# Two 64-query attention tiles of neighbouring heads as one tile of 128 rows, in a fused attention and feed-forward kernel

## The chip, the cores and the metric

One core of one Trainium2 chip. The time is the device time of the whole program in microseconds (us). Three runs of the kernel before gave 1238.19, 1238.35 and 1239.01; their median, 1238.35, is the time before. One further execution was profiled.

## What is computed

Eight batches of eight heads, 576 positions, 64 numbers a head, all in float32. Each head's output mixes causal softmax attention with a linear memory; the mix is one input row of a two-layer feed-forward part with 512 inputs and 2048 hidden units.

```python
scores = q @ k.T / sqrt(64), causal;  a = softmax(scores);  local = a @ v
phi(x) = where(x > 0, x, exp(x) - 1) + 1
mem = (phi(q) @ M_prev) / (phi(q) @ z_prev + 1e-6)
g = 1 / (1 + exp(-beta))                  # one number a head
x = g * mem + (1 - g) * local             # heads side by side: 4608 x 512
out = leaky_relu(x @ w_in, 0.01) @ w_out  # 512 -> 2048 -> 512
```

## The kernel before

**Chunks and heads.** A batch's 576 queries are two chunks: chunk 0 has the first 320 queries (and needs the first 320 keys), chunk 1 the other 256 (and all 576 keys). Work goes unit by unit: batch `b`, chunk `hf`, head `h`. Chunk 0 has three tiles of 64, 128 and 128 query rows with 64, 192 and 320 keys; chunk 1 has two of 128 rows with 448 and 576 keys (`ROWS`, `KEYS`, lines 35 to 39).

**One head** (`attention`, line 361). One DMA loads a block `raw` of 128 partitions: transposed q and k, then M and v in blocks of 128 rows, z, and q by rows (line 355). The first two chunks, both of batch 0, are "plain" and compute in float32. All later ones split each operand into a high and a low part and multiply the parts with faster matmuls: ACT casts q and k (line 395), POOL makes the low part of q (line 402) and of k on 64 partitions (line 399), and the same for v (lines 408, 412). For each tile PE makes the scores with two matmuls (line 530) into `s`; DVE adds the mask and takes the row's minimum of the negated scores (line 534) into `pp`; ACT takes the exponential and its sum (line 550); DVE adds the gate to the sum, inverts it and scales the row (lines 555, 560, 563). POOL writes the memory part, phi(q) divided by its norm, into the first 64 columns of `pp` (line 566). Then PE transposes blocks of 128 columns of `pp` into `t` (line 479), ACT casts them into the high half of `pt` (line 494) and DVE subtracts for the low half (line 497). When all of the head's blocks are there, PE multiplies them with M and v (line 664) into `o`, and ACT, DVE and POOL make x and its low part from it (lines 667 to 676). The small chain on phi(q) (lines 433 to 452) runs beside this, for all tiles of a head at once.

**The 64-row tile.** Its scores are two matmuls of 64 columns, and its `pp` has 64 columns of memory part and 64 of probabilities, so its transpose is one block. A block of 128 rows, transposed, gives 128 columns of which the copies take 64 (`ROWS[0]`).

**Feed-forward part** (class `Moe`, line 688). For a chunk that is done: 16 steps, each with 12 matmuls into `h` and 12 into `acc` (line 699), over 320 or 256 columns, with the weights also split in high and low parts.

**Order.** Every instruction is recorded as an `op` with an engine, a duration from a small table, a priority and the tiles that it reads and writes. `Plan.issue` (line 127) then runs a list schedule over those durations and writes the program of each engine in that order; at run time each engine goes through its own list and waits on semaphores. Attention has the better priority; the feed-forward matmuls of the chunk before fill PE. `Buf` gives tiles in rings: two of `raw`, `qk`, `pp`, `pt` and the PSUM tile `t`, one of `vt`; a new user of a ring waits for the last reader of the one that had its place. An operation that DVE shares a port for is planned not to overlap with one of POOL (`port=True`).

Of the kernel before, what the change touches and what calls it, by code (L numbers as in the profile page):

```python
# [20 lines left out]
P = 128  # L21
# [11 lines left out]
RAWW = (320 + 320 + 3 * 64 + 64 + 3 * 64, 256 + 576 + 5 * 64 + 64 + 2 * 64)  # L33

# [184 lines left out]
def moe_attention(ctx, tc, raw0, raw1, beta, w_in, w_out, out, nb):  # L219
    nc = tc.nc  # L220
    rawd = (raw0, raw1)
    pool = lambda name, **kw: ctx.enter_context(tc.tile_pool(name=name, bufs=1, **kw))
# [57 lines left out]
    nc.vector.tensor_scalar(out=gate[:, 1, :], in0=gate[:, 1, :], scalar1=1.0e18, scalar2=None, op0=ALU.min)  # L280
    pts = []
# [65 lines left out]
    def load(b, hf, h, prio):  # L347
        args = [P, RAWW[1]], F32, "raw", 2, f"raw{b}_{hf}_{h}"
        if (b, hf) == (0, 0) and h % 2:
            r = c0_tile([P, RAWW[0]], F32, "rawc0", 2, args[4])  # L350
        elif (b, hf) == (0, 1) and h % 2:
            r = c1_tile(*args[:2], "rawc1", 1, args[4])
        else:
            r = tile_(*args)
        op("DMA", RAWW[hf] * 512 / 310, prio, lambda: nc.sync.dma_start(r()[:, : RAWW[hf]], rawd[hf][b, h]), w=[r[0]])
        raws[b, hf, h] = r

    xs = {}
    x32s = {}

    def attention(b, hf, h, prio):
        u = f"{b}_{hf}_{h}"
        nq, nk, tl, nj = NQ[hf], NK[hf], TILES[hf], NJ[hf]
        ni = len(tl)
        raw = raws.pop((b, hf, h))
        o_v, o_z, o_q = nq + nk, nq + nk + nj * D, nq + nk + nj * D + D

        full = plain(b, hf)
        if not full:
            qk = late_tile([P, 1088], F32R, "qk", 2, "qk" + u)  # L370
# [13 lines left out]
        else:  # L384

            pt = plan.buf(None, None, None, "pt", 2, None, behind["late"])
            pt.make = lambda at=pt.at: pt_tile(at % 2)
# [6 lines left out]
        def qk_hi():  # L394
            nc.scalar.copy(qk()[:, : nq + nk], raw()[:, : nq + nk])  # L395

        def k_lo():
            ks = slice(nq, nq + nk)
            nc.gpsimd.tensor_tensor(out=qk()[64:, ks], in0=raw()[64:, ks], in1=f32r_bits(qk()[64:, ks]), op=ALU.subtract)

        def q_lo():
            nc.gpsimd.tensor_tensor(out=qk()[:, nq + nk : nk + 2 * nq], in0=raw()[:, :nq], in1=f32r_bits(qk()[:, :nq]), op=ALU.subtract)
# [13 lines left out]
        else:  # L416
            operands = [qk["q"], qk["k"], qk["ql"]]
            op("ACT", act(nq + nk), prio, qk_hi, r=[raw[0]], w=[qk["q"], qk["k"]])
            op("POOL", pool_(nq), prio, q_lo, r=[raw[0], qk["q"]], w=[qk["ql"]])
            op("POOL", pool_(nk), prio, k_lo, r=[raw[0]], w=[qk["k"]])  # L420
# [20 lines left out]
        def phi_z():  # L441
            z = raw()[:, o_z:o_q].unsqueeze(1).to_broadcast([P, ni, D])
# [5 lines left out]
        def phi_den():  # L448
            nc.vector.tensor_scalar(out=rn(), in0=rn(), scalar1=1e-6, scalar2=gate[:, 0, h : h + 1], op0=ALU.add, op1=ALU.mult)
# [23 lines left out]
        def turns(ii, i, rw, n, pp):  # L473
            for j0, js in BLOCKS[i]:
# [6 lines left out]
                def part(x, js=js, i=i, rw=rw):  # L481
# [8 lines left out]
                def tv(t=t, js=js, rw=rw):  # L490
                    return t()[:, : len(js) * rw].rearrange("p (j q) -> p j q", q=rw)

                def p_hi(part=part, tv=tv):
                    nc.scalar.copy(part(0), tv())  # L494

                def p_lo(part=part, tv=tv):
                    nc.vector.tensor_tensor(out=part(1), in0=tv(), in1=f32r_bits(part(0)), op=ALU.subtract)  # L497
# [7 lines left out]
        for ii, i in enumerate(tl):  # L505
# [13 lines left out]
            for k, (k0, kc, kn) in enumerate(PIECES[i]):  # L519
                s = bank(("acc0", "s", "acc1")[i] if (b, hf) == (0, 0) else "s", 1, f"s{u}_{i}_{k}")  # L520

                def score(s=s, i=i, k0=k0, kc=kc, kn=kn):
                    if full:
# [3 lines left out]
                        return  # L527
                    for k in range(2):
                        c = COL[i] + k * (nq + nk)
                        nc.tensor.matmul(s()[:, :kc], qk()[:, c : c + P], qk()[:, nq + k0 : nq + k0 + kc], start=k == 0, stop=k == 1)  # L530

                def top(s=s, i=i, k=k, k0=k0, kn=kn, pp=pp, stat=stat):
                    mo = S - KEYS[i] + k0 if i else S - P
                    nc.vector.tensor_tensor_reduce(  # L534
                        out=pp()[:, D + k0 : D + k0 + kn],
                        in0=s()[:, :kn],
                        in1=mask[:, mo : mo + kn],
                        scale=-0.0625 if full else -0.125,
                        scalar=stat(k - 1) if k else 3.0e38,
                        op0=ALU.add,  # L540
                        op1=ALU.min,
                        accum_out=stat(k),
                    )

                op("PE", pe4(kn) if full else 2 * pe(kc), prio, score, r=operands, w=[s[0]])
                op("DVE", dve_top(kn) + 60 * (k > 0), prio, top, r=[s[0], st["m", ii, k - 1]], w=[pp["s", k], st["m", ii, k]])
# [7 lines left out]
            def inv(stat=stat):  # L554
                nc.vector.tensor_scalar(
                    out=stat(2), in0=stat(2), scalar1=1e-9, scalar2=gate[:, 1, h : h + 1], op0=ALU.add, op1=ALU.mult
                )
# [58 lines left out]
        blocks = [(i, j0) for i in tl for j0, _ in BLOCKS[i]]  # L616
# [43 lines left out]
        c0 = [min(0 if j < tl[0] or j == 0 else COL[j], nq - 192) for j in range(nj)]  # L660
# [152 lines left out]
def layout(q, k, v, M_prev, z_prev, beta, moe_w_in, moe_w_out):  # L813
# [9 lines left out]
    raw1 = np.concatenate([qT[..., 320:], kT, vx, zb, qx[..., 3 * D :]], -1)  # L823
    wi = moe_w_in.reshape(4, P, NF, P).transpose(2, 1, 0, 3).reshape(NF, P, DM)
# [29 lines left out]
```

## Time and profile before

| | before |
|---|---|
| median of 3 runs | 1238.35 us |
| the profiled execution, own time | 1238.4 us |
| its span, first to last instruction | 1236.6 us |
| PE busy | 1204.7 us (97%), 8936 matmuls |
| DVE, ACT, POOL busy | 827.7, 831.7, 707.4 us |
| bytes moved by DMA | 107.57 MB, mean 87 GB/s |

The engines run beside each other, so the busy times don't add up. PE is TensorE's matmuls, PEld its weight loads, DVE is VectorE, ACT ScalarE, POOL GpSimd, SP the engine that issues the DMAs. Matmuls are pipelined: the duration of one row runs into the next, so what one costs is read from starts. "Idle before" is the time an engine stood before an instruction, with the one that ended the wait.

### The profile page before, as it was taken

How to read it: one execution, taken by the hardware profiler on the slowest of the kernel's cores; microseconds unless marked ns; L12 is line 12 of the kernel's file. 1: busy time of each engine (PE TensorE's matmuls, PEld its weight loads, DVE VectorE, ACT ScalarE, POOL GpSimd, SP SyncE). 2: the span in 40 equal slices, each digit the busy share in tenths (PEclk: the TensorE clock that was granted, in tenths of full speed). 3: DMA queues.
4: the chain of work that ended last, by engine and by line, in shares of the span. 5: the costliest groups of instructions: out<-in, count | busy, mean ns of one | idle time of the engine just before them, and what ended most of it. 6: DMA issues, size and time to landing. Idle time of an engine off the chain costs nothing.

```text
span 1236.6 us, 25876 instructions
## 1 busy us (share of the span) xinstructions
PE 1204.7 (97%) x8936; PEld 1159.9 (94%) x8936; DVE 827.7 (67%) x2836; ACT 831.7 (67%) x2451; POOL 707.4 (57%) x1064
## 2 busy tenths in 40 slices
PE   6699999999999999999999999999999999999998
PEld 4488899999999999999999999999999999999998
DVE  6989877778687747767476775767567674776100
ACT  7877777777767757677576765767577775767322
POOL 1022276676776656666476665757666675766222
PEclk9999999999999999999999999999999999999999
DMA  6555322222323212222122221222122221222000
GB/s 248 185 177 171 126 95 82 85 86 74 98 69 108 73 47 93 76 96 73 59 87 76 91 73 59 90 86 78 55 81 90 86 73 48 93 79 74 1 22 18
DMA packets 32530, 107.57 MB, mean 87 GB/s; under 512 B 3728, under 2 KB 11920, under 8 KB 32400
## 3 DMA queue, kind: packets, MB, share of 16 engines
q1 hardware_dynamic: 32400, 105.92, 26.0%
q8 instruction: 71, 1.16, 0.4%
q14 instruction: 59, 0.48, 0.1%
HBM read 96.47 MB, written 9.44 MB: 86 GB/s over the span
## 4 chain that ended last, share of the span: by engine, by line
PE 88%; DVE 4%; ACT 4%; DMA 1%; POOL 1%; issue 1%; SPq 0%; POOLq 0%; DVEq 0%
PE acc L699 31%; PE h L699 31%; PE t L479 8%; PE o L664 8%; PE s L530 7%; PE o L628 2%; DMA raw<-raw 1%; PE s L526 1%; ACT pp L550 1%; DVE pp L534 1%; ACT gh L726 1%; ACT qk L395 1%; DVE pp L563 1%; ACT g L727 0%; DVE ph L439 0%
## 5 line engine op out<-in xcount | busy, mean ns | idle before, releaser
L732 POOL TENSOR_TENSOR gl<-g,gh 128x320 fp32r<-128x320 f32 (+1 forms) x256 | 210.3, 822 | 247.8 <-ACT g L727 220.8
L699 PE MATMUL h<-xh,wih 128*128 128x256 f32 (+1 forms) x1024 | 321.9, 314 | 3.7 <-ACT g L727 2.6
L699 PE MATMUL acc<-gh,woh 128*128 128x256 f32 (+1 forms) x1024 | 316.2, 309 | 0.0
L699 PE MATMUL h<-xl,wih 128*128 128x256 f32 (+1 forms) x1024 | 302.1, 295 | 0.4 <-DVE xl L648 0.4
L699 PE MATMUL h<-xh,wil 128*128 128x256 f32 (+1 forms) x1024 | 302.3, 295 | 0.0
L699 PE MATMUL acc<-gl,woh 128*128 128x256 f32 (+1 forms) x1024 | 301.5, 294 | 0.0
L699 PE MATMUL acc<-gh,wol 128*128 128x256 f32 (+1 forms) x1024 | 301.4, 294 | 0.0
L550 ACT ACTIVATE pp<-pp,st 128x448 f32<-128x448 f32 (+3 forms) x320 | 180.6, 565 | 85.2 <-DVE st L534 80.4
L699 PEld LDWEIGHTS h<-xh,wih 128*128 128x128 f32 x1024 | 194.1, 190 | 7.9 <-ACT g L727 4.2
L726 ACT ACTIVATE gh<-h 128x320 fp32r<-128x320 f32 (+1 forms) x256 | 104.8, 409 | 143.4 <-PE h L699 141.5
L699 PEld LDWEIGHTS h<-xl,wih 128*128 128x128 f32 x1024 | 194.1, 190 | 2.1 <-issue 0.9
L699 PEld LDWEIGHTS acc<-gl,woh 128*128 128x128 f32 x1024 | 193.3, 189 | 0.8 <-POOL gl L732 0.2
L699 PEld LDWEIGHTS acc<-gh,woh 128*128 128x128 f32 x1024 | 193.0, 188 | 0.8 <-issue 0.2
L699 PEld LDWEIGHTS h<-xh,wil 128*128 128x128 f32 x1024 | 193.1, 189 | 0.0
L699 PEld LDWEIGHTS acc<-gh,wol 128*128 128x128 f32 x1024 | 192.5, 188 | 0.0
L497 DVE TENSOR_TENSOR pt<-t,pt 128x256 fp32r<-128x256 f32 (+4 forms) x392 | 161.4, 428 | 37.7 <-ACT pt L494 34.5
L494 ACT CAST pt<-t 128x256 fp32r<-128x256 f32 (+4 forms) x392 | 142.2, 382 | 60.8 <-PE t L479 58.6
L479 PE MATMUL t<-ident,pp 128*128 128x128 f32 x960 | 169.4, 277 | 9.6 <-DVE pp L563 2.7
L534 DVE CUSTOM_DVE_ANT_0 pp<-s,mask 128x448 f32<-128x448 f32 (+3 forms) x320 | 137.7, 431 | 46.8 <-PE t L479 22.7
L563 DVE TENSOR_SCALAR pp<-pp,st 128x64 f32<-128x64 f32 (+4 forms) x280 | 150.5, 538 | 7.1
L530 PE MATMUL s<-qk 128*128 128x320 f32 (+4 forms) x672 | 151.5, 307 | 1.0 <-DVE st L534 0.2
L479 PEld LDWEIGHTS t<-ident,pp 128*128 128x128 f32 x960 | 116.4, 141 | 23.1 <-ACT pt L494 5.2
(67 smaller groups left out, 2042.7 us busy)
## 6 DMA issues: line engine op xcount, KB each, us to landing
raw<-raw SPq DMA_DIRECT2D x64, 672.0 KB, 4.0
raw<-raw SPq DMA_DIRECT2D x64, 544.0 KB, 3.6
wrwi<-w_in_bits SPq DMA_DIRECT2D x16, 512.0 KB, 3.5
wrwo<-w_out_bits SPq DMA_DIRECT2D x16, 512.0 KB, 3.6
out_t<-os SPq DMA_DIRECT2D x32, 160.0 KB, 1.8
out_t<-os SPq DMA_DIRECT2D x32, 128.0 KB, 1.8
braw<-beta_b SPq DMA_DIRECT2D x1, 4.0 KB, 1.6
```

The costliest lines, as they stand in the source:

```text
L479: nc.tensor.transpose(t()[:, (j - j0) * P : (j - j0 + 1) * P], pp()[:, j * P : (j + 1) * P], ident)
L494: nc.scalar.copy(part(0), tv())
L497: nc.vector.tensor_tensor(out=part(1), in0=tv(), in1=f32r_bits(part(0)), op=ALU.subtract)
L530: nc.tensor.matmul(s()[:, :kc], qk()[:, c : c + P], qk()[:, nq + k0 : nq + k0 + kc], start=k == 0, stop=k == 1)
L534: nc.vector.tensor_tensor_reduce(out=pp()[:, D + k0 : D + k0 + kn], in0=s()[:, :kn], in1=mask[:, mo : mo + kn], scale=-0.0625 if full else ...
L550: nc.scalar.activation(out=pp()[:, D : D + n], in_=pp()[:, D : D + n], func=AF.Exp, scale=-1.0, bias=stat(kl_), accum_out=stat(2))
L563: nc.vector.tensor_scalar(out=pp()[:, D : D + n], in0=pp()[:, D : D + n], scalar1=stat(2), scalar2=None, op0=ALU.mult)
L628: nc.tensor.matmul(o()[a, c0[j] : nq], v, pt()[:, 0, cols(j, c0[j]) : cols(j, nq)], start=j == 0, stop=j == nj - 1)
L664: nc.tensor.matmul(o()[:, c0[j] : nq], vt()[:, j, :], pt()[:, t, cols(j, c0[j]) : cols(j, nq)], start=n == 0, stop=n == len(mm) - 1)
L699: nc.tensor.matmul(dst(), l(), r(), start=start and k + j == 0, stop=stop and k + j == len(ops) - 1)
L726: op("ACT", act(n, True), q, lambda: nc.scalar.activation(out=gh()[:, :n], in_=hp()[:, :n], func=AF.Prelu, alpha=0.01), r=[hp[0]], w=[gh[0]])
L732: lambda: nc.gpsimd.tensor_tensor(out=gl()[:, :n], in0=g()[:, :n], in1=f32r_bits(gh()[:, :n]), op=ALU.subtract),
```

## The change

In the 320-query chunk of batches 1 to 7 (`paired`), the 64-query tile of an even head and that of the odd head behind it become one tile of 128 rows, worked on with the even head: the odd head's queries in rows 0 to 63, the even head's in rows 64 to 127. The host lays out a further input, `rawp`, one block for each pair of heads: the even head's block with the odd head's first 64 queries and keys put ahead of the even head's own, and three blocks of z. The even head loads this block (1344 columns where it loaded 1088), and its q and k parts are 384 columns long, not 320. The pair's scores are two matmuls of 128 columns, of which the off-diagonal quarters are not used; the mask and minimum go over each half of the rows by itself. One exponential, one scaling, one memory part and one transpose follow. The transposed block's columns are copied in two parts, to the even head's `pt` and to the odd head's. The even head takes its tiles in the order 1, 2, then the pair's; the odd head has tiles 1 and 2 alone. Two small constants hold the gates by halves of the rows, made by five copies at the start.

```diff
@@ layout, on the host
+    ev, od = slice(0, None, 2), slice(1, None, 2)
+    half = np.arange(P)[:, None] < D
+    zp = np.where(half, zb[:, od], zb[:, ev])
+    qp = np.where(half, qx[:, od, :, :D], np.roll(qx[:, ev, :, :D], D, 2))
+    rawp = np.concatenate(
+        [
+            *(qT[:, od, :, :D], qT[:, ev, :, :320], kT[:, od, :, :D], kT[:, ev, :, :320], vx[:, ev, :, : 3 * D]),
+            *(zp, zb[:, ev], zb[:, ev], qp, qx[:, ev, :, D : 3 * D]),
+        ],
+        -1,
+    )
@@ load
+        two = paired(b, hf) and h % 2 == 0
+        src, n = (rawp[b, h // 2], RAWP) if two else (rawd[hf][b, h], RAWW[hf])
@@ attention
+        if paired(b, hf) and h % 2:
+            tl = tl[1:]
...
+            pt = pairs.pop(b) if paired(b, hf) and h % 2 else new_pt()
+            if two:
+                pt2 = pairs[b] = new_pt()
...
-                op("ACT", act(nn, True), prio, p_hi, r=[t[0]], w=[pt["h", i, j0]])
-                if not full:
-                    op("DVE", dve(nn), prio, p_lo, r=[t[0], pt["h", i, j0]], w=[pt["l", i, j0]])
+                for to, c in ((pt, 64), (pt2, 0)) if two and i == 0 else ((pt, 0),):
...
+                    op("ACT", act(nn, True), prio, p_hi, r=[t[0]], w=[to["h", i, j0]])
+                    if not full:
+                        op("DVE", dve(nn), prio, p_lo, r=[t[0], to["h", i, j0]], w=[to["l", i, j0]])
+        order = list(enumerate(tl))
+        if two:
+            order = order[1:] + order[:1]
...
+                    c, w, n = (0, wq, P) if two and i == 0 else (q0 + COL[i], wq + k0_ + k0, kc)
                     for k in range(2):
-                        c = COL[i] + k * (nq + nk)
-                        nc.tensor.matmul(s()[:, :kc], qk()[:, c : c + P], qk()[:, nq + k0 : nq + k0 + kc], start=k == 0, stop=k == 1)
+                        ql = qk()[:, c + k * (wq + wk) : c + k * (wq + wk) + P]
+                        nc.tensor.matmul(s()[:, :n], ql, qk()[:, w : w + n], start=k == 0, stop=k == 1)
...
+                    for rs, c in ((slice(0, 64), 0), (slice(64, P), 64)) if two and i == 0 else ((slice(0, P), 0),):
+                        nc.vector.tensor_tensor_reduce(
+                            out=pp()[rs, D + k0 : D + k0 + kn],
+                            in0=s()[rs, c : c + kn],
+                            in1=mask[rs, mo + c : mo + c + kn],
...
```

The scheduler writes a new order behind the plain chunks. In the names below, `s_0_2_0_0` is chunk 0, head 2, tile 0, and the last number is a buffer's. PE, the scores of a small tile in the chunk 0 of batch 6, as they stand before (head 3's):

```order
L699 MATMUL h_0_10_13200<-xl_0_0_11253,wih_1306 128x320
L699 MATMUL h_0_10_13200<-xh_0_0_11239,wil_1310 128x320
L530 MATMUL s_0_3_0_0_13227<-qk_0_3_13151 128x64 x2
L479 MATMUL t_0_2_1_0_13234<-ident,pp_0_2_1_13161 128x128 x2
L699 MATMUL acc_0_0_12494<-gh_0_9_13170,woh_1270 128x320
L699 MATMUL acc_0_0_12494<-gl_0_9_13186,woh_1270 128x320
```

And with the change, in the same chunk, those of the pair of heads 2 and 3:

```order
L747 MATMUL acc_0_2_12320<-gl_0_8_12895,woh_1170 128x320
L747 MATMUL acc_0_2_12320<-gh_0_8_12882,wol_1181 128x320
L577 MATMUL s_0_2_0_0_12972<-qk_0_2_12849 128x128 x2
L747 MATMUL acc_0_3_12328<-gh_0_8_12882,woh_1170 128x320
L747 MATMUL acc_0_3_12328<-gl_0_8_12895,woh_1170 128x320
L747 MATMUL acc_0_3_12328<-gh_0_8_12882,wol_1181 128x320
L520 MATMUL t_0_2_1_0_12981<-ident,pp_0_2_1_12938 128x128 x2
```

Head 3 has no such row any more. In the whole program PE has 616 score matmuls for 672 and 932 transposes for 960; between a pair's scores and its transpose stand 18 to 48 feed-forward matmuls, and between the last products of the odd head before and that transpose 18 to 72.

DVE in the same chunk with the change, where the pair's tile goes through: two reductions of 64 rows, then one gate, one reciprocal and one scaling (its `pp_0_2_0`), beside the other tiles of heads 2 and 3:

```order
L583 ISA pp_0_2_0_12990,st_0_2_12912<-s_0_2_0_0_12972,mask 64x64
L583 ISA st_0_2_12912 64x1
L583 ISA pp_0_2_0_12990,st_0_2_12912<-s_0_2_0_0_12972,mask 64x64
L583 ISA st_0_2_12912 64x1
L542 TENSOR_TENSOR pt_1990<-t_0_2_1_0_12981,pt_1990 128x2x128
L484 TENSOR_REDUCE st_0_3_13006<-pz_0_3_12934 128x2
L605 TENSOR_SCALAR st_0_2_12912<-st_0_2_12912,gpair 128x1
L490 TENSOR_SCALAR st_0_3_13006<-st_0_3_13006,gate 128x2
L608 RECIPROCAL st_0_2_12912<-st_0_2_12912 128x1
L583 ISA pp_0_3_1_13018,st_0_3_13006<-s_0_3_1_0_13003,mask 128x192
L583 ISA st_0_3_13006 128x1
L611 TENSOR_SCALAR pp_0_2_0_12990<-pp_0_2_0_12990,st_0_2_12912 128x64
```

Before, each of the heads had its own such tile here, with one reduction of 128 rows, a gate, a reciprocal and a scaling.

## Rows read from the trace of the kernel before

**Rows 1.** The page's span, the busy time of each engine (share of the span, instructions), and the shares of the chain that ended last.
```profile
span 1236.6 us, 25876 instructions
PE 1204.7 (97%) x8936; PEld 1159.9 (94%) x8936; DVE 827.7 (67%) x2836; ACT 831.7 (67%) x2451; POOL 707.4 (57%) x1064
PE 88%; DVE 4%; ACT 4%; DMA 1%; POOL 1%; issue 1%; SPq 0%; POOLq 0%; DVEq 0%
```

**Rows 2.** The stretches view: 155 to 1154 us, from the end of the plain chunks to the end of the last attention. Columns: length, busy us and instructions of PE, PEld, DVE, ACT and POOL, granted clock, DMA share, GB/s.
```profile
155.00:1154.00 999.00, 991.77 (x7602) 975.98 (x7602) 696.72 (x2458) 689.76 (x2049) 657.50 (x997) 1.00 0.24 78
```

**Rows 3.** The waits of PE in that stretch, the longest sum: who waited for whom, us in total, times, the longest.
```profile
PE t L479 <- DVE pp L563: 2.7, 5, 0.6
```

**Rows 4.** Single rows in order of time (start, duration, engine, line): the last x of the 320-query chunks of batches 1 and 3 on POOL, and the first feed-forward matmuls of the chunks of batches 1, 3 and 7 on PE.
```profile
220.02 0.88 POOL L676 TENSOR_TENSOR xl<-x,xh 128x320 fp32r<-128x320 f32 x1
...
228.58 0.31 PE L699 MATMUL h<-xh,wih 128*128 128x320 f32 x1
...
498.20 0.88 POOL L676 TENSOR_TENSOR xl<-x,xh 128x320 fp32r<-128x320 f32 x1
...
527.52 0.30 PE L699 MATMUL h<-xh,wih 128*128 128x320 f32 x1
...
1114.44 0.31 PE L699 MATMUL h<-xh,wih 128*128 128x320 f32 x1
```

**Rows 5.** PE in order of time, three places: one transpose, two scores of 192 columns, two of 64 columns ("x2": two in one row), each between feed-forward matmuls of 320 columns. Between 443.37 and 446.74 there are only feed-forward matmuls, 23 steps.
```profile
429.50 0.31 PE L699 MATMUL acc<-gh,wol 128*128 128x320 f32 x1
429.65 0.27 PE L479 MATMUL t<-ident,pp 128*128 128x128 f32 x1
429.68 0.40 PE L699 MATMUL h<-xh,wih 128*128 128x320 f32 x1
429.91 0.31 PE L699 MATMUL h<-xl,wih 128*128 128x320 f32 x1
...
432.27 0.31 PE L699 MATMUL acc<-gh,wol 128*128 128x320 f32 x1
432.41 0.37 PE L530 MATMUL s<-qk 128*128 128x192 f32 x2
432.62 0.33 PE L699 MATMUL acc<-gh,woh 128*128 128x320 f32 x1
432.79 0.31 PE L699 MATMUL acc<-gl,woh 128*128 128x320 f32 x1
...
443.37 0.31 PE L699 MATMUL acc<-gh,woh 128*128 128x320 f32 x1
...
446.74 0.30 PE L699 MATMUL acc<-gh,wol 128*128 128x320 f32 x1
446.88 0.30 PE L530 MATMUL s<-qk 128*128 128x64 f32 x2
447.02 0.40 PE L699 MATMUL acc<-gh,woh 128*128 128x320 f32 x1
447.25 0.31 PE L699 MATMUL acc<-gl,woh 128*128 128x320 f32 x1
```

**Rows 6.** Groups of instructions by line and shape: count, busy us, mean ns of one, idle time before them. Score matmuls of 64 columns, and the weight loads of all score matmuls.
```profile
L530 PE MATMUL s<-qk 128*128 128x64 f32 x112 | 19.0, 252 | 0.2
L530 PEld LDWEIGHTS s<-qk 128*128 128x128 f32 x672 | 104.9, 189 | 6.0 <-DVE st L534 3.2 <-POOL pz L443 0.9 <-POOL qk L399 0.3
```

**Rows 7.** The same view, other engines: casts of q and k, low parts, exp and memory part of the 64-row tile (L566 has one shape for all tiles).
```profile
L395 ACT CAST qk<-raw 128x832 fp32r<-128x832 f32 x56 | 49.9, 890 | 8.2 <-DMA raw<-raw 8.2
L395 ACT CAST qk<-raw 128x640 fp32r<-128x640 f32 x56 | 40.7, 726 | 12.2 <-DMA raw<-raw 11.3 <-PE acc L699 0.8
L399 POOL TENSOR_TENSOR qk<-raw,qk 64x320 fp32r<-64x320 f32 x56 | 49.5, 884 | 4.4
L402 POOL TENSOR_TENSOR qk<-raw,qk 128x320 fp32r<-128x320 f32 x56 | 49.2, 879 | 29.6 <-ACT qk L395 25.0 <-PE t L479 2.8 <-PE o L664 0.6
L402 POOL TENSOR_TENSOR qk<-raw,qk 128x256 fp32r<-128x256 f32 x56 | 42.6, 761 | 41.0 <-ACT qk L395 27.1 <-PE t L479 12.4 <-PE h L699 1.4
L550 ACT ACTIVATE pp<-pp,st 128x64 f32<-128x64 f32 x64 | 22.4, 350 | 12.5 <-DVE st L534 11.0 <-DVE st L560 0.9
L566 POOL TENSOR_TENSOR pp<-ph,st 128x64 f32<-128x64 f32 x280 | 86.9, 314 | 67.6 <-PE t L479 23.5 <-DVE st L452 21.0 <-DVE st L560 7.4
```

**Rows 8.** The page's DMA issues: the loads of `raw`, count, KB each, median us from issue to landing.
```profile
raw<-raw SPq DMA_DIRECT2D x64, 672.0 KB, 4.0
raw<-raw SPq DMA_DIRECT2D x64, 544.0 KB, 3.6
```

**Rows 9.** DVE in order of time at the start, the idle time ahead of a row in brackets.
```profile
2.90 0.17 DVE L280 TENSOR_SCALAR gate<-gate 128x8 f32<-128x8 f32 x1
6.27 0.36 DVE L439 SCALAR_TENSOR_TENSOR ph<-ph,pz 128x192 f32<-128x192 f32 x1 [3.20 <-ACT pz L436]
```

**Rows 10.** POOL, DVE and PE in order of time at 767 us.
```profile
766.86 0.87 POOL L399 TENSOR_TENSOR qk<-raw,qk 64x320 fp32r<-64x320 f32 x1
766.91 0.99 DVE L563 TENSOR_SCALAR pp<-pp,st 128x320 f32<-128x320 f32 x1
767.24 0.28 PE L699 MATMUL h<-xh,wil 128*128 128x256 f32 x1
768.05 0.57 PE L479 MATMUL t<-ident,pp 128*128 128x128 f32 x3 [0.54 <-DVE pp L563]
```

More of the change, by code (lines that the diff above doesn't have):

```diff
@@ L216, in pool_, with moe_attention, paired @@
     return 135 + 2.175 * n
-def moe_attention(ctx, tc, raw0, raw1, beta, w_in, w_out, out, nb):
+def moe_attention(ctx, tc, raw0, raw1, rawp, beta, w_in, w_out, out, nb):
     nc = tc.nc
     rawd = (raw0, raw1)
+    def paired(b, hf):
+        return not hf and not plain(b, hf)
     pool = lambda name, **kw: ctx.enter_context(tc.tile_pool(name=name, bufs=1, **kw))
@@ L280, in moe_attention @@
     nc.vector.tensor_scalar(out=gate[:, 1, :], in0=gate[:, 1, :], scalar1=1.0e18, scalar2=None, op0=ALU.min)
+    gpair = cst.tile([P, 2, H // 2], F32, name="gpair")
+    gden = cst.tile([P, H // 2, 3], F32, name="gden")
+    for k in range(2):
+        rows = slice(64 * (1 - k), 64 * (2 - k))
+        nc.vector.tensor_copy(out=gpair[rows], in_=gate[rows].rearrange("p k (g t) -> p k g t", t=2)[:, :, :, k])
+    nc.vector.tensor_copy(out=gden[:, :, 0:1], in_=gpair[:, 0, :].unsqueeze(2))
+    for k in range(1, 3):
+        nc.vector.tensor_copy(out=gden[:, :, k : k + 1], in_=gate[:, 0, :].rearrange("p (g t) -> p g t", t=2)[:, :, 0:1])
     pts = []
@@ L359, in moe_attention @@
     x32s = {}
+    pairs = {}
     def attention(b, hf, h, prio):
@@ L363, in attention @@
         nq, nk, tl, nj = NQ[hf], NK[hf], TILES[hf], NJ[hf]
+        two = paired(b, hf) and h % 2 == 0
+        if paired(b, hf) and h % 2:
+            tl = tl[1:]
         ni = len(tl)
         raw = raws.pop((b, hf, h))
-        o_v, o_z, o_q = nq + nk, nq + nk + nj * D, nq + nk + nj * D + D
+        q0 = k0_ = D if two else 0
+        wq, wk = nq + q0, nk + k0_
+        o_v = wq + wk
+        o_z = o_v + nj * D
+        o_q = o_z + (3 if two else 1) * D
+        if paired(b, hf) and h % 2:
+            o_q += D
         full = plain(b, hf)
         if not full:
-            qk = late_tile([P, 1088], F32R, "qk", 2, "qk" + u)
+            qk = late_tile([P, 1152], F32R, "qk", 2, "qk" + u)
             vt = late_tile([P, 5, P], F32R, "vt", 1, "vt" + u)
@@ L384, in attention, with new_pt @@
         else:
-            pt = plan.buf(None, None, None, "pt", 2, None, behind["late"])
-            pt.make = lambda at=pt.at: pt_tile(at % 2)
+            def new_pt():
+                pt = plan.buf(None, None, None, "pt", 2, None, behind["late"])
+                pt.make = lambda at=pt.at: pt_tile(at % 2)
+                return pt
+            pt = pairs.pop(b) if paired(b, hf) and h % 2 else new_pt()
+            if two:
+                pt2 = pairs[b] = new_pt()
         w = ni * D
@@ L448, in phi_den @@
         def phi_den():
+            if two:
+                nc.vector.scalar_tensor_tensor(out=rn(), in0=rn(), scalar=1e-6, in1=gden[:, h // 2, :], op0=ALU.add, op1=ALU.mult)
+                return
             nc.vector.tensor_scalar(out=rn(), in0=rn(), scalar1=1e-6, scalar2=gate[:, 0, h : h + 1], op0=ALU.add, op1=ALU.mult)
@@ L552, in exp, with inv @@
                 )
[L554 to L557, printed above, removed]
+            def inv(stat=stat, i=i):
+                g = gpair[:, 1, h // 2 : h // 2 + 1] if two and i == 0 else gate[:, 1, h : h + 1]
+                nc.vector.tensor_scalar(out=stat(2), in0=stat(2), scalar1=1e-9, scalar2=g, op0=ALU.add, op1=ALU.mult)
             def inv2(stat=stat):
@@ L659, in attention @@
         mm = [(j, t) for j in range(nj) for t in range(2)]
-        c0 = [min(0 if j < tl[0] or j == 0 else COL[j], nq - 192) for j in range(nj)]
+        c0 = [min(0 if j < TILES[hf][0] or j == 0 else COL[j], nq - 192) for j in range(nj)]
         def pv():
```

59 lines of the change are left out of this document (30 added, 29 removed).

## Prediction

> **What bounds the kernel now.** I read the page's totals first, then one row of the stretches view, then the waits of TensorE, then single rows in order of time. The totals show TensorE (PE) busy for 1204.7 of 1236.6 us, while VectorE (DVE), ScalarE (ACT) and GpSimd (POOL) stand at 57 to 67%; the chain that ended last runs through PE for 88% of the span [rows 1]. Behind the two plain chunks, from 155 us to the end of the last attention, PE is busy 991.77 of 999 us at a granted clock of 1.00, that is 2.4 GHz; the other three have 302 to 342 us free in the same stretch [rows 2]. So what PE no longer has to do there should come off the time, if nothing else becomes late. The waits in which PE stood idle in that stretch are few and short; the largest sum is 2.7 us, in 5 waits for a row block that DVE scales [rows 3].
>
> Is the attention late for the feed-forward part? The last x of a 320-query chunk is written at 220.02 + 0.88 = 220.9 us and the first matmul that reads that chunk's x starts at 228.58; two batches further on it is 499.08 and 527.52 [rows 4]. The attention is 8 to 28 us ahead. Four batches later the same first matmul stands at 1114.44: a batch takes 146.7 us [rows 4]. What makes a pair of heads slower by a microsecond only eats into that lead; what makes PE itself stand at an instruction costs time at once, because its order is fixed.
>
> **What a small tile costs PE.** A matmul's own duration on this chip's rows overlaps with the next one, so I take starts. Between 443.37 and 446.74 us PE issues 23 steps of 320-column matmuls: 3.37 / 23 = 0.1465 us each [rows 5]. Two score matmuls of 64 columns stand between 446.74 and 447.25; take away the two 320-column steps that lie in the same stretch (0.293) and 0.51 - 0.293 = 0.217 us is left for both. The same for 192 columns: 432.79 - 432.27 - 0.293 = 0.227. For a single transpose: 429.91 - 429.50 - 0.293 = 0.117 [rows 5].
>
> So three times the columns cost 0.010 us more: such a matmul is paid by the piece, not by the column. The rows of the weight loads say why that can be: every score matmul, whatever its width, has a load of 128x128 (672 of them, 189 ns each) [rows 6]. The new score tile has 128 columns, between the two measured widths; its bounds are 0.217 and 0.227 us for two, and I take 0.22, nearer to the width it is nearer to.
>
> **The sum on PE.** The pairing applies to the 320-query chunk of batches 1 to 7, four pairs of heads each: 28 pairs. Each had two 64-query tiles, that is 112 score matmuls in all [rows 6], and now has one of 128 rows.
> - Scores: two tiles cost 2 x 0.217, one costs 0.22. Saved 0.214 us a pair, 6.0 us in all.
> - Transposes: one instead of two, 0.117 us a pair, 3.3 us in all.
> - The products with V, and everything of the feed-forward part, keep their number and shape.
>
> Together 28 x 0.331 = 9.3 us. With the upper bound it is 28 x 0.324 = 9.1, with the lower 9.4, so the price of the new width hardly matters.
>
> The Trainium skill speaks against the larger half of this. Its page "TensorE: Matmul & The Clock Gate", section "Back-to-back issue gap", gives an isolated matmul about 60 cycles for up to 64 columns and 134 cycles for 128: at 2.4 GHz, 25 ns and 56 ns. By it four matmuls of 64 columns (100 ns) would be cheaper than two of 128 (112 ns), and only the transpose would be gained, an estimate of 28 x (56 - 12) ns = 1.2 us, ending at 1237.2. The same section says that pairs of load and matmul do not follow that form, and this case's rows side with that: 0.217 us for two, not 0.05.
>
> **What the other engines do, and why I cost it at nothing.** Per pair, ACT loses an exp of 64 columns (350 ns and the reading of its sum) and a third of the odd head's small phi block; its cast of q and k grows by 128 columns, which from 726 ns at 640 and 890 at 832 is 109 ns more [rows 7]. POOL loses one memory product of 314 ns; q's low part grows by 64 columns (879 ns at 320 against 761 at 256, so 118 more) and k's low part from 884 to at most 884 x 384 / 320 = 1061 ns [rows 7]. So POOL is lighter by some 20 ns a pair before the smaller phi block, ACT by more. DVE loses a scaling of 64 columns and two short operations on the row sums; its score reductions become two of 64 rows for the one of 128 that each was paired from, so two per pair as before, and fewer rows make them no cheaper: k's low part on 64 rows costs 884 ns where q's on 128 rows costs 879 [rows 7]. The odd head's first 64 rows of the transpose go to the other buffer, still two casts and two subtractions per pair. All of this lies beside PE, under 302 us or more of free time on each engine [rows 2]; if that cover were gone, POOL's longer q and k parts of even heads, 28 x 0.295 = 8.3 us, would be the first to show.
>
> The load of an even head grows from 544 to 672 KB. The trace has loads of both sizes: 3.6 and 4.0 us from issue to landing [rows 8], so 0.4 us more, and it is issued a head ahead; DMA is busy 0.24 of the stretch [rows 2]. SP issues as many loads as before, in the same order but for one that moves past a few stores of the output. The five small copies of the gates at the start stand on DVE between 3.07 us and 6.27 us, where it is idle for 3.20 us; at the 0.17 us of the gate's own operation they take 0.85 [rows 9]. Nothing there.
>
> One wait is new. The even head now also writes the odd head's buffer of probabilities, which the odd head of the pair before must have finished reading. In the new order of PE, between the last products of that head and the pair's transpose stand at least 18 feed-forward matmuls, 18 x 0.12 = 2.2 us or more, so I cost it at nothing. If it came late, PE would stand at the odd head's next transposes, whose buffers of PSUM the waiting casts hold.
>
> **Size of what I can't work out.** The planner writes a wholly new order for every engine behind the plain chunks, and PE's stalls depend on it. At 767 us one is to be seen: a scaling of 320 columns on DVE began at 766.91 and took 0.99 us, beside k's low part on POOL (766.86 + 0.87), and PE started the transpose that needs it at 768.05 where its last matmul had started at 767.24: 0.81 us for a step of 0.12, a stall of 0.69 [rows 10]. The order repeats from batch to batch, so such a misfit comes once per batch: 7 x 0.69 = 4.8 us, gained if one goes, lost if one comes. That gives the forecast its own range.
>
> **The number.** The profiled execution took 1238.4 us, of which 1.8 lie outside the span; the median of the three runs is 1238.35, so nothing is to be converted. 1238.4 - 9.3 = **1229.1**, with 1224.3 to 1233.9 as the forecast's own range (one misfit less or more per batch).
>
> **Rivals.**
> 1. *The score matmuls cost by the column.* At 0.1465 / 320 = 0.46 ns a column, four of 64 and two of 128 cost the same, and only 28 x 0.117 = 3.3 us go: 1235.1. Against it stand the two widths at 0.217 and 0.227 us. Chance 0.03.
> 2. *The gain is given back by new stalls.* Two misfits more per batch, each like that at 767 us, cost 7 x 2 x 0.69 = 9.7 us: 1238.8, no change. For it: the order is new everywhere and the low parts of even heads hold POOL longer. Against it: DVE has less to do in each pair, and the planner counts the new lengths. Chance 0.06.
> 3. *Slower: the pair's scaling waits for POOL each time.* The pair's tile is now the last one of the even head, just where the next head's q and k parts run on POOL. If its scaling on DVE, and so its transpose on PE, met such a part in every pair, PE would stand 0.69 us as at 767 us and 0.17 more for the longer part: 28 x 0.86 = 24.1 us lost against 9.3 won, 1253.2. It decides from 0.331 us of stall a pair on. For it: the mechanism is in the trace [rows 10]. Against it: only 5 such waits of PE in 999 us now [rows 3], and in the new order 18 to 48 feed-forward matmuls, at least 2.2 us, stand between the pair's scores and its transpose. Chance 0.05.
>
> That the change doesn't do what it says is excluded: the order of PE has 84 matmuls fewer, 56 of scores and 28 transposes, and 56 score matmuls of 128 columns where 112 of 64 stood.
>
> **How the numbers follow.** Forecast 0.86, rivals 0.03, 0.06 and 0.05. A measurement of this kernel can tell about 0.2%, 2.5 us, from no change. Faster by more than that are the forecast and rival 1: 0.89. Within it, rival 2: 0.06. Slower, rival 3: 0.05. The range goes from the low end of the forecast to just past rival 1, 1224.0 to 1235.5, which leaves out rivals 2 and 3 (0.11) and a little of the forecast's edges.
>
> **What would show it.** Score matmuls of 128 columns, 56 of them, with about 0.22 us net for two between feed-forward matmuls; 28 transposes fewer at 0.117; PE idle in the attention stretch still near 7 us; the period of one batch, now 146.7 us, shorter by 4 x 0.331 = 1.3 us. It is wrong if two matmuls of 128 columns cost over 0.3 us net, if PE's waits for scaled rows grow to more than 10 us, or if the first feed-forward matmul of a chunk waits for x.

## The result, and the profile after

The change made the kernel slower: 1246.01 us (median of 4, 1243.67 to 1248.03) against 1238.57 (median of 4, 1238.19 to 1239.01). The ratio is 1.0051, with 1.0031 to 1.0071 as its 95% interval, so some 6 us lost (7.4 between the medians) where 9.3 were to be won. The profiled execution took 1245.25 us.

The page of the changed kernel, against [rows 1]:

```profile
span 1243.0 us, 25603 instructions
PE 1200.3 (97%) x8852; PEld 1150.9 (93%) x8852; DVE 828.0 (67%) x2757; ACT 819.8 (66%) x2395; POOL 704.9 (57%) x1036
PE 81%; DVE 8%; ACT 5%; DMA 3%; issue 1%; POOL 1%; SPq 0%; ACTq 0%; POOLq 0%; DVEq 0%
```

PE has the 84 matmuls fewer and 4.4 us less busy time, and yet the span is 6.4 us longer. The chain says where to look: PE's share fell from 88 to 81%, DVE's rose from 4 to 8.

The stretch from 155 to 1154 us (columns as in [rows 2]), and the waits of PE from 155 to 1140 us (as in [rows 3]: us in total, times, the longest):

```profile
155.00:1154.00 999.00, 981.52 (x7480) 961.53 (x7479) 694.51 (x2371) 676.38 (x1990) 654.64 (x968) 1.00 0.25 82
```

```profile
PE t L520 <- DVE pp L611: 8.1, 10, 1.1
PE h L747 <- ACT g L775: 2.9, 3, 1.0
PE t L520 <- DVE x L718: 2.4, 6, 0.6
PE s L577 <- DVE st L583: 1.3, 4, 0.5
```

PE is busy 981.52 of 999 us where it was 991.77: idle time went from 7.2 to 17.5 us, at the same clock of 1.00 and nearly the same DMA share. Waits of a transpose for a scaled row block grew from 2.7 to 8.1 us. The same from PE's starts, which need no modelled ends: give every matmul behind 155 us the regular step of its shape (0.147 us for 320 columns, 0.110 for a transpose, and so on), and what is left of the time is waiting. Work fell from 1055.7 to 1047.8 us (76 matmuls fewer, not 84, lie behind 155 us), waiting rose from 22.5 to 36.8: -7.9 and +14.3 make the 6.4 us of the span.

The price of the new tile is where it was put. PE in order of time, a pair's two scores of 128 columns:

```profile
282.32 0.31 PE L747 MATMUL acc<-gh,wol 128*128 128x320 f32 x1
282.47 0.33 PE L577 MATMUL s<-qk 128*128 128x128 f32 x2
282.64 0.36 PE L747 MATMUL acc<-gh,woh 128*128 128x320 f32 x1
282.83 0.31 PE L747 MATMUL acc<-gl,woh 128*128 128x320 f32 x1
```

282.83 - 282.32 - 0.293 = 0.217 us for both; over 22 such places the median is 0.223.

Where the waits are. POOL, DVE and PE at 978 us, in the 256-query chunk of batch 6, whose heads have no pairs:

```profile
978.62 0.31 PE L747 MATMUL h<-xh,wil 128*128 128x320 f32 x1
978.65 1.20 DVE L611 TENSOR_SCALAR pp<-pp,st 128x576 f32<-128x576 f32 x1
978.67 0.87 POOL L447 TENSOR_TENSOR vt<-raw,vt 128x320 fp32r<-128x320 f32 x1 [1.01 <-ACT vt L443]
980.00 0.52 PE L520 MATMUL t<-ident,pp 128*128 128x128 f32 x3 [1.07 <-DVE pp L611]
```

PE starts a matmul at 978.62 and the next, head 4's transpose, at 980.00: 1.38 us for a step of 0.147. The scaling that it waits for took 1.20 us beside v's low part on POOL. It is the mechanism of [rows 10], at another operation and nearly twice as long (1.23 us late for 0.69), and it comes once a batch; the same scaling in three batches before:

```profile
537.85 1.20 DVE L611 TENSOR_SCALAR pp<-pp,st 128x576 f32<-128x576 f32 x1
684.79 1.20 DVE L611 TENSOR_SCALAR pp<-pp,st 128x576 f32<-128x576 f32 x1
831.70 1.19 DVE L611 TENSOR_SCALAR pp<-pp,st 128x576 f32<-128x576 f32 x1
```

Five batches lose some 1.2 us each at this one transpose; two more of the same chunk (heads 0 and 2) lose about 0.7 and 0.5. All PE steps that ran over 0.15 us late sum to about 23 us for 13 before, and some 14 of the 23 are transposes of the 256-query chunk. The forms of the scaling (count, busy us, mean ns of one, idle before):

```profile
L611 DVE TENSOR_SCALAR pp<-pp,st 128x576 f32<-128x576 f32 x56 | 47.0, 839 | 1.1
L611 DVE TENSOR_SCALAR pp<-pp,st 128x448 f32<-128x448 f32 x56 | 33.1, 590 | 1.1
L611 DVE TENSOR_SCALAR pp<-pp,st 128x320 f32<-128x320 f32 x56 | 28.2, 503 | 1.6
L611 DVE TENSOR_SCALAR pp<-pp,st 128x64 f32<-128x64 f32 x28 | 13.0, 463 | 0.2
```

and the first of these forms as it was before, 186 ns shorter in the mean:

```profile
L563 DVE TENSOR_SCALAR pp<-pp,st 128x576 f32<-128x576 f32 x56 | 36.6, 653 | 1.6
```

It is not that more scalings meet POOL. Counted over all widths, 88 took over 0.2 us more than the shortest of their width before and 87 after; all the scalings together are 46.8 and 48.2 us longer than at their shortest. They are others: of 576 columns 16 before and 31 after, of 320 columns 29 and 15, and now PE stands right behind them. The pair's own tile has the last row, 15 of 28 stretched, but PE's late steps are not mainly there.

### The profile page after: what moved, and what is told of

It reads as the page before. It is cut to its first block, busy times and chain, and to the rows that moved or that the text cites. A ratio compares the mean times of both kernels' runs of the same rounds, so it can differ in the third digit from the quotient of the medians.

```text
span 1243.0 us, 25603 instructions
## 1 busy us (share of the span) xinstructions
PE 1200.3 (97%) x8852; PEld 1150.9 (93%) x8852; DVE 828.0 (67%) x2757; ACT 819.8 (66%) x2395; POOL 704.9 (57%) x1036
## 4 chain that ended last, share of the span: by engine, by line
PE 81%; DVE 8%; ACT 5%; DMA 3%; issue 1%; POOL 1%; SPq 0%; ACTq 0%; POOLq 0%; DVEq 0%
PE acc L747 29%; PE h L747 28%; PE t L520 7%; PE o L712 7%; PE s L577 6%; PE o L676 2%; DVE pp L611 2%; DMA raw<-raw 2%; PE s L572 1%; ACT pp L599 1%; DVE pp L583 1%; DVE pt L542 1%; DMA raw<-rawp 1%; DVE x L718 1%; ACT os L813 1%
## 5 line engine op out<-in xcount | busy, mean ns | idle before, releaser
L599 ACT ACTIVATE pp<-pp,st 128x320 f32<-128x320 f32 (+4 forms) x292 | 171.4, 587 | 88.7 <-DVE st L583 82.2
L520 PE MATMUL t<-ident,pp 128*128 128x128 f32 x932 | 164.3, 277 | 18.4 <-DVE pp L611 8.1
L542 DVE TENSOR_TENSOR pt<-t,pt 128x256 fp32r<-128x256 f32 (+4 forms) x392 | 158.9, 428 | 32.3 <-ACT pt L539 29.5
L611 DVE TENSOR_SCALAR pp<-pp,st 128x448 f32<-128x448 f32 (+3 forms) x252 | 146.8, 582 | 5.6
L577 PE MATMUL s<-qk 128*128 128x320 f32 (+4 forms) x616 | 144.1, 315 | 1.3 <-DVE st L583 1.3
L520 PEld LDWEIGHTS t<-ident,pp 128*128 128x128 f32 x932 | 109.8, 141 | 34.9 <-POOL vt L447 10.1
```

The lines of the kernel that those rows point to most:

```text
L520: nc.tensor.transpose(t()[:, (j - j0) * P : (j - j0 + 1) * P], pp()[:, j * P : (j + 1) * P], ident)
L542: nc.vector.tensor_tensor(out=part(1, pt=to), in0=tv(c=c), in1=f32r_bits(part(0, pt=to)), op=ALU.subtract)
L577: nc.tensor.matmul(s()[:, :n], ql, qk()[:, w : w + n], start=k == 0, stop=k == 1)
L599: nc.scalar.activation(out=pp()[:, D : D + n], in_=pp()[:, D : D + n], func=AF.Exp, scale=-1.0, bias=stat(kl_), accum_out=stat(2))
L611: nc.vector.tensor_scalar(out=pp()[:, D : D + n], in0=pp()[:, D : D + n], scalar1=stat(2), scalar2=None, op0=ALU.mult)
```

## The experiments

All ratios are to the kernel before, run beside it, with 95% intervals.

**Is it the order, and if so its tightness?** The planner takes every PE operation of attention behind the plain chunks as ready 1.0 us later than its inputs from other engines, so that other matmuls are put ahead of it. Nothing else changes; one kernel from before, one from after.

```diff
+late = 1000 if o.eng == "PE" and 62 <= o.prio < 100000 else 0
-o.ready = max((d.end + latency(d.eng, o.eng) for d in o.deps), default=0)
+o.ready = max((d.end + latency(d.eng, o.eng) + (0 if d.eng == "PE" else late) for d in o.deps), default=0)
```

> The kernel before, with one change in the planner: behind the plain chunks it takes every attention instruction of PE as ready 1.0 us later than its inputs, so that the feed-forward matmuls that stand ready are put ahead of it. No instruction changes, only the order. Theory A (PE loses its time at transposes and scores whose inputs come later than planned; any attention has 8 to 28 us of lead to give away): the waits of PE in the attention stretch, now 7 us idle, go to under 3, and the time falls by 5 to 15 us, to 1223 to 1233. Theory B (the pairing itself makes attention late, the order of the kernel before is sound): within 3 us of 1238.

> The changed kernel with the same 1.0 us in the planner. Theory A (the 9.3 us of PE work are saved, and an order full of misfits gives back 16): most misfits go, and the kernel comes out 9 us (7 to 11) below the kernel before with the same slack, so 1214 to 1224. Theory B (longer low parts, the wait for the odd head's buffer, the pair's tile as the last one hold up the heads): it stays within 3 us of the kernel before with slack, or above it, with waits at the pair's own transposes.

Before with it: 1233.31 us, 0.9949 [0.9928, 0.9969], as theory A has it; but in its trace PE is idle 12.6 us from 155 to 1154 us (999 - 986.44), not under 3, nearly all of it at the feed-forward part (the execution in the trace took 1237.65 us, the longest of the four). After with it: 1226.43, 0.9901 [0.9882, 0.9919], 19.6 us below the changed kernel as it was made, and 2.4 above the 1224 that was expected at most. The waits of PE in this second kernel, 155 to 1140 us:

```profile
PE h L748 <- ACT g L776: 8.7, 11, 2.3
PE h L748 <- POOL xl L725: 1.1, 1, 1.1
PE s L578 <- POOL qk L435: 0.7, 1, 0.7
```

No transpose is waited for any more, while 71 scalings are still stretched (mean 669 ns at 576 columns). So stretched scalings need not cost time: they do where PE stands behind them. What comes late next is the feed-forward part itself, the activations between its two products. Slack gives the old kernel 6 us as well: it had stalls of this kind too. With slack in both, pairing saves 6.9 us.

**Which operations?** The same 1.0 us, but only behind DVE's operations that share POOL's port, which, among those that feed PE there, are the scalings, and so ahead of the transposes behind them:

```diff
+... + (late if d.eng == "DVE" and d.port else 0) for d in o.deps), default=0)
```

> The changed kernel; the planner takes an attention instruction of PE as ready 1.0 us later only where its input comes from an operation of DVE that shares the port with POOL, which is the scaling of a row block ahead of its transposes; scores and products with V keep their times. If the misfits are scalings stretched beside POOL (theory A, the port): nearly all of the gain of the full 1.0 us comes back, 1225 to 1231. If the misfits are spread over scores, products and transposes alike: about half, 1234 to 1240. If the pairing itself delays heads: no less than 1243.

1229.33 us, 0.9935 [0.9909, 0.996]: 16.7 of the 19.6 us between the medians, 14.4 of 18.6 by the ratios. Its longest waits of PE:

```profile
PE s L578 <- DVE st L584: 3.2, 6, 0.6
PE h L748 <- ACT g L776: 2.7, 4, 1.0
```

The row of waits for scalings is gone, and most of what the full slack gives comes with it, as was expected if the scalings are the place of the loss. This, too, is a new order as a whole; but it was changed only where the loss was said to sit. For the kernel as it was made, that the loss sits mainly at transposes behind scalings is therefore shown.

**Taking the contention away.** The scaling as a DVE operation with the factor broadcast along the row, and planned without the shared port:

```diff
-nc.vector.tensor_scalar(out=pp()[:, D : D + n], in0=pp()[:, D : D + n], scalar1=stat(2), scalar2=None, op0=ALU.mult)
+nc.vector.tensor_tensor(out=pp()[:, D : D + n], in0=pp()[:, D : D + n], in1=stat(2).to_broadcast([P, n]), op=ALU.mult)
-op("DVE", dve2(n), ..., port=True)
+op("DVE", dve(n), ...)
```

> The changed kernel with the scaling of the rows as a two-operand multiply with the factor broadcast, planned at its longer duration and without the port that DVE shares with POOL; the planner writes yet another order. Theory A, part 2 (the misfits come from scalings that stretch to 1.0 to 1.7 us when they meet an operation of POOL): no scaling above 0.85 us, PE's 8.1 us of waits for scaled rows fall below 3, and the time falls by 5 us or more, below 1241. If the misfits have another source: the scalings are even but PE waits as much, 1243 or more.

It came out slower: 1273.7 us, 1.0282 [1.0264, 1.03].

```profile
L611 DVE TENSOR_TENSOR pp<-pp,st 128x576 f32<-128x576 f32 x56 | 55.9, 998 | 1.7
```

```profile
PE t L520 <- POOL pp L614: 7.5, 20, 0.8
```

This form is stretched too (576 columns from 753 to 2026 ns), so dropping the planner's rule only let more of them meet, and now POOL's memory part is held up as well (20 waits). It says nothing against the theory, and took nothing away.

**The price of a score matmul.** The kernel before in its own order, but the scores of a 64-row tile are one matmul, not two (the second, with the low part of q, is left out): 56 matmuls less, one for each of the 56 small tiles.

```diff
-for k in range(2):
+parts = 2 if i else 1
+for k in range(parts):
...
-    start=k == 0, stop=k == 1)
+    start=k == 0, stop=k == parts - 1)
```

> The kernel before, its planner's durations and so its order of work unchanged, but the score of each 64-row tile behind the plain chunks is one matmul, not two (the product with the low part of q is left out for that tile): 56 matmuls of 64 columns less. Theory A (PE's work is the bound, and a small matmul is worth 0.11 us whatever its width): 6.1 us less, 1232.3, give or take 1.5. If PE's work in the small tiles is hidden by waits for other engines: no more than 2 us less. If matmuls are paid by the column (0.03 us each): 1.6 us less.

1234.06 us, 0.996 [0.9946, 0.9975], 5.3 us less than the kernel before it ran beside. The group of these scores:

```profile
L531 PE MATMUL s<-qk 128*128 128x64 f32 x56 | 12.7, 226 | 0.3 <-DVE pt L497 0.2
```

5.3 / 56 = 0.095 us a matmul, near the 0.1085 of [rows 5]: with the order unchanged, PE's work does come off the time.

**Where the tile stands.** The change also moves the pair's tile behind the even head's other two. Here the pair's tile comes first again:

```diff
-order = order[1:] + order[:1]
+order = order[:]
```

> The changed kernel with the pair's tile first in the even head, as the 64-row tile stood before, not last. Theory B (the pair's tile as the last one, its wait for the odd head's buffer, makes the even head late): the loss goes, 1229 to 1234. Theory A (the order is full of misfits by chance): another order with other misfits, anywhere from 1232 to 1250, and its waits again lie mostly in heads of the 256-query chunk, which the pairing does not touch.

1231.81 us, 0.9956 [0.9938, 0.9973]: faster than before, and some 12 us faster than the change as made by the ratios (14 between the medians). It has the same longer loads, casts and low parts as the change as made, so these by themselves are not what lost the time. Its waits of PE, and the 576-column scaling:

```profile
PE t L520 <- DVE pp L611: 2.1, 6, 1.1
PE t L520 <- DVE x L718: 1.3, 1, 1.3
```

```profile
L611 DVE TENSOR_SCALAR pp<-pp,st 128x576 f32<-128x576 f32 x56 | 42.5, 760 | 1.7
```

**Or is it only luck?** A new order of any kind may fall well or badly. To draw other orders of the same kernel I changed a number that decides nothing of the work, the time that the planner allows behind a POOL operation: 45 ns as it is, and 30, 60, 75.

```diff
-BEHIND = {"PE": 165, "ACT": 102, "DVE": 75, "POOL": 45, "DMA": 2000}
+BEHIND = {"PE": 165, "ACT": 102, "DVE": 75, "POOL": 60, "DMA": 2000}
```

First at 60, in the kernel before (b_jit) and in the changed one (a_jit):

> The kernel before with one number of the planner changed by 15 ns (the time from the end of a POOL operation to a reader's start, 45 to 60 ns), which changes nothing but the order. Theory A: the order is a lot drawn anew; the waits of PE differ from those of before, and the time lies 3 us or more from 1238.5 on either side, most likely above (the kernel before has few misfits). If orders of this planner are all about alike: within 2.5 us of 1238.5.

> The changed kernel with the same 15 ns in the planner. Theory A: another lot; 3 us or more from 1245.5, most likely below, since its misfits are many, and 9 us below the other kernel only on the mean over such lots. If the pairing itself costs 16 us of waits: within 3 us of 1245.5.

Then 30 and 75 in both:

> The kernel before with the planner's number for POOL at 30 ns. Theory A: a lot of its own; with 1238.5 at 45 and 1243.0 at 60, anywhere from 1236 to 1246. If the kernel before is a picked lot, above 1238.5.

> As the run at 30 ns, with 75: 1236 to 1246, above 1238.5 if the kernel before is a picked lot. The mean of the kernel before over its four lots, less the mean of the kernels with the tile first over three, is what the pairing is worth: by the PE work 9.3 us, by theory A 6 to 12.

> The changed kernel with the planner's number for POOL at 30 ns (45 as changed, 60 in the run before this). If the pair's tile as the last one costs by its nature (theory B): 1242 to 1249 again, with or without the number. If each order is a lot (theory A): spread wider, 1230 to 1250, its long waits at other tiles than in the other two.

> As the run at 30 ns, with 75. Theory B: 1242 to 1249. Theory A: anywhere from 1230 to 1250.

And with the pair's tile first:

> As the run before, with 30 ns. Theory B: within 3 us of 1231.8. Theory A: anywhere from 1230 to 1250.

> The pair's tile first in the even head, with the planner's number at 60 ns. Theory B (first is better by nature): within 3 us of the 1231.8 at 45 ns. Theory A: anywhere from 1230 to 1250, and the mean over the kernels with the tile first is no more than 4 us below that with the tile last.

The fourth corner is the kernel before, unpaired, with the even heads' small tile last, at 45 and then at 30 and 60:

```diff
+order = list(enumerate(tl))
+if not full and not hf and h % 2 == 0:
+    order = order[1:] + order[:1]
-for ii, i in enumerate(tl):
+for ii, i in order:
```

> The kernel before, without pairing, with the 64-row tile of each even head of the 320-query chunks behind the plain ones taken last, not first. If the place of the tile is the cause (theory B): 1246 to 1254, the 8 to 16 us that the place costs in the paired kernel. If it is the lot that each order is (theory A): 1236 to 1246, like the kernel before with another lot.

> The unpaired kernel with the small tile of even heads last, and the planner's number for POOL at 30 ns. If the place costs by its nature (theory B, as the first lot of it at 1245.8 says): 1243 to 1250, above the 1237.7 that the kernel before has with this number. If the 1245.8 was a bad lot (theory A): 1236 to 1243.

> As the run before, with 60 ns. Theory B: 1243 to 1252, above the 1243.0 that the kernel before has with this number. Theory A: 1236 to 1243.

Median us, ratio and interval:

| planner's POOL number | 30 | 45 | 60 | 75 |
|---|---|---|---|---|
| not paired, tile first (before) | 1237.66, 0.9991 [0.9978, 1.0004] | 1 | 1243.04, 1.0048 [1.0029, 1.0068] | 1240.8, 1.0014 [1.0004, 1.0025] |
| not paired, tile last | 1249.15, 1.0078 [1.0055, 1.0101] | 1245.77, 1.0054 [1.0039, 1.0069] | 1240.57, 1.0011 [0.9998, 1.0024] | |
| paired, tile first | 1229.09, 0.9927 [0.9911, 0.9944] | 1231.81, 0.9956 [0.9938, 0.9973] | 1228.52, 0.9933 [0.9914, 0.9953] | |
| paired, tile last (after) | 1247.15, 1.0077 [1.0057, 1.0097] | 1246.01, 1.0051 [1.0031, 1.0071] | 1245.15, 1.0067 [1.0043, 1.009] | 1234.41, 0.9966 [0.9951, 0.9981] |

Means over the three common numbers: 1.0013, 1.0048, 0.9939, 1.0065. The order alone moves a kernel by 5.4, 8.6, 3.3 and 12.7 us (the four rows), so one kernel's result is one draw. Even so, pairing with the tile first is faster at all three numbers, by 0.0074 in the mean, 9.2 us (5.4 to 14.2). Tile last is dearer by 0.0035 (4.3 us) unpaired, though not at 60, and by 0.0126 (15.6 us) paired, at each of the three numbers (11.8 to 18.6). With the tile last, pairing wins nothing in the mean of the three. The draw at 75 stands outside these means, as two of the rows have none there, and in it the changed kernel is faster than before; so the 15.6 us are a size from three draws. Of the two theories in these expectations, B (the place costs by its nature) is borne out by the paired kernel at 30, 45 and 60 and the unpaired one at 30, A (each order is a lot) by the paired kernel at 75 and the unpaired one at 60: both are at work.

PE's waits for scaled row blocks go the same way, but not in every draw. They are 0.7 to 2.7 us in the seven kernels with the tile first; 10.9, 5.4 and 2.8 us unpaired with the tile last (30, 45, 60); 9.6, 8.1, 0.9 and 1.4 us in the changed kernel (30, 45, 60, 75). The changed kernel at 60 is as slow as at 45 with 0.9 us of them. By the profile PE waits elsewhere there, for DVE's gate on the row sums and for its score minima:

```profile
PE t L520 <- DVE st L605: 6.2, 6, 1.1
PE s L577 <- DVE st L583: 5.4, 15, 0.9
```

So stretched scalings are the main loss of the change as made, and not of every slow order.

In the unpaired kernel with the tile last (at 45) the 576-column scaling is longer as well, 798 ns for 653, so the move alone can do that:

```profile
L566 DVE TENSOR_SCALAR pp<-pp,st 128x576 f32<-128x576 f32 x56 | 44.7, 798 | 1.9
```

**Both together.** The pair's tile first and the 1.0 us of slack:

> The pairing with its tile first, and the 1.0 us in the planner. Theory A: PE's waits for attention are gone whatever the place, so the place matters no more: within 3 us of the 1226.4 with the tile last. Theory B: 4 us or more below that.

1222.91 us, 0.9876 [0.985, 0.9901]: faster than both kernels. Its waits of PE, all of them over 0.5 us:

```profile
PE h L748 <- ACT g L776: 7.8, 10, 2.0
PE h L748 <- ACT xh L722: 2.0, 1, 2.0
PE h L748 <- POOL xl L725: 0.6, 1, 0.6
```

With slack the place is worth 0.0025 (3.1 us), within what the two intervals allow. Against the old kernel with slack pairing saves 0.0073, 9.0 us.

## Why the prediction was wrong

- **What bounds the kernel: right.** PE does, and PE's order is fixed, so what it waits for costs time at once. That sentence of the prediction is what then happened.
- **The sum on PE: right.** Two scores of 128 columns cost 0.217 to 0.223 us for the 0.22 taken; PE's work fell by 7.9 us in the one trace; pairing saved 9.2 us in the mean of three orders with the tile first (5.4 to 14.2 in the single ones), 9.0 with slack and the tile first, and 6.9 with slack and the tile last, for 9.3. The Trainium skill's page "TensorE: Matmul & The Clock Gate", section "Back-to-back issue gap", would have an isolated 64-column matmul cost 25 ns, and leaving out 56 of them an estimated 1.4 us. The 5.3 us measured go with the row and with that page's own reservation on pairs of load and matmul.
- **The work of the other engines, the loads and the gates at nothing: not contradicted.** The loads of the new size land after 4.0 us as read off, PE's waits at `h` are for the activation and not for x, and its one wait for a `pt` is 0.2 us. The chain's share of DMA rose from 1 to 3%, but it is 3% in a_port too, which is fast.
- **The step that failed: "Size of what I can't work out".** It put one misfit like that at 767 us more or less per batch, 0.69 us each, 4.8 in all, with no side preferred. The changed kernel has three in each of five batches (1.2, 0.7 and 0.5 us), and 14.3 us of waiting more in all. The prediction had the right mechanism, had its row, and took a single wait's size and a count of one for the spread of a wholly new order. Even its own row did not come seven times: the wait for a scaled block is there 5 times [rows 3]. The spread could be had by drawing orders: 3.3 to 12.7 us within a kernel, at its most larger than the gain. That the change came out slower, and not only less fast, is in part the draw: at 75 it is faster than the kernel before.
- **A second one: the moved tile costed at nothing.** "The pair's tile is now the last one of the even head" stood in a rival and not in the sum. The runs give the move 4.3 us unpaired (a tendency: two numbers of three) and 15.6 paired (three of three, but only three draws), and 3.1 with slack, which may be nothing.
- **Rival 3 had the side and the mechanism, but not the place.** It asked for a stall at the pair's own scaling in every pair. The waits lie mainly at other heads' transposes, in the 256-query chunk, where the change touches no instruction. Rival 2, two misfits more in each batch, came nearest in kind; the 14.3 us are three of its size (14.3 / 7 / 0.69).
- **"What would show it" told the two apart.** The limit of 10 us on waits for scalings was not reached (8.1), but PE's idle time was to stay near 7 us and is 17.5. And the batch period did not shrink: the first feed-forward matmul of batches 1, 3 and 7's 320-query chunks now stands here ([rows 4] has 228.58, 527.52 and 1114.44):

```profile
233.60 0.31 PE L747 MATMUL h<-xh,wih 128*128 128x320 f32 x1
...
530.92 0.31 PE L747 MATMUL h<-xh,wih 128*128 128x320 f32 x1
...
1119.78 0.31 PE L747 MATMUL h<-xh,wih 128*128 128x320 f32 x1
```

(1119.78 - 530.92) / 4 = 147.2 us a batch, where 146.7 less 1.3 was expected.

**What stays open.** It is open whether the tile's place really costs three times as much with pairing as without (15.6 us for 4.3, from three draws each), and if so, why. One explanation is argued only: the even head writes the first part of the odd head's buffer of probabilities, so with the pair's tile last the odd head's copies can be planned only behind the even head's very last transpose, and everything of two heads gets closer together. It was not tried. Nor is it shown which instruction makes the planner put the 256-query chunk's scalings beside v's low part.

## What to carry to other kernels

Where one engine runs a fixed order at 97%, a change that takes work from it is worth that work only if the new order stalls no more than the old; draw a few orders of both kernels (any number of the planner that changes no work will do) before believing either sign of a difference of half a per cent. Stretched operations on other engines are harmless until the bound engine stands right behind them, so a little planned slack ahead of just those (here 1.0 us behind the scalings, worth 14 to 17 us) can be worth more than the change itself. And cost the moved position of a step, not only its instructions.

## What the runs showed of the hardware

- **A scaling that meets POOL and waits ends a fixed time after it.** In the changed kernel 576-column scalings take about 0.51 us alone. Those that began 0.02 us or less around the start of v's low part (0.86 to 0.88 us) took 1.19 to 1.20; those where the low part of the activations (0.73 to 0.75 us) began 0.01 us behind them took 1.05 to 1.07; each ends some 0.32 us behind POOL's operation. For 448, 320 and 64 columns that wait the same stretch behind POOL is 0.25, 0.18 and 0.05 us. Where POOL began 0.12 to 0.13 us behind the scaling's start, as here, the scaling took 0.51 as if alone:

```profile
951.81 0.51 DVE L611 TENSOR_SCALAR pp<-pp,st 128x576 f32<-128x576 f32 x1
951.94 0.99 POOL L437 TENSOR_TENSOR qk<-raw,qk 128x256 fp32r<-128x256 f32 x1 [1.37 <-ACT qk L430]
```

So one that shows the earlier start can still be the one that waits, and 0.1 us between two starts decide over 0.67 us on DVE.
- The Trainium skill's page "SBUF — State Buffer", section "Who interferes with whom", says that a DVE operation in a two-port mode contends with GpSimd, that whichever issues first holds the shared pair for its whole instruction, and that the other blocks. The rows agree that one waits for all of the other. Which is first is not what the profile's start says: at 978.65 DVE's row starts 0.02 us ahead, and DVE is the one that waited (POOL's spans are rough, so the 0.02 is not certain).
- The same section says that a DVE operation with two inputs in SBUF contends with a GpSimd operation that reads SBUF. The broadcast form agrees: 753 ns at its shortest for 576 columns, 998 in the mean.
- **A kernel's own time spreads by more than its first four runs show.** The first four runs of the kernel before lie 0.8 us apart, those of the changed kernel 4.4. But the 63 runs of the kernel before beside the experiments, on five chips, go from 1235.69 to 1242.61 us: 45 at a mean granted clock of 0.997 took 1238.4 in the mean, 14 at 0.994 took 1240.7. The changed kernel's 1243.67, 1245.25 and 1248.03 all show 0.997, so the clock is not all of it; what the rest is stays open.
